# Wider tiles in two chained MoE layers behind a local attention, on one core

## The chip, the cores and the metric

One core of a Trainium2 chip runs the whole kernel. The metric is the device time of one execution in microseconds, launch to end; the kernel before was run three times. The profiled execution is a single one, and its span (first to last instruction) is a little shorter than its time.

## What is computed

Everything is float32. Attention: 4 batches, 8 heads, 768 tokens of 64 channels, in chunks of 32 queries; each chunk sees 16 tokens to its left, itself, 8 to its right and 8 memory tokens. Its output, 3072 tokens of 512 channels, goes through two feed-forward layers:

```python
h = x @ w_in                    # 512 -> 2048
x = (np.maximum(h, 0) ** 2) @ w_out          # -> 512
g, val = x @ w_gate, x @ w_val  # 512 -> 1536 each
out = (g / (1 + np.exp(-g)) * val) @ w_out2  # -> 512
```

## The kernel before

**Numbers as pairs.** A float32 operand is split into a high part in a format that TensorE takes at full rate (float32r) and a low remainder, and each product is three passes: high by high, high by low, low by high. The split is a copy on ScalarE and a subtraction on VectorE or GpSimd (`split`, L94). The weights come as 64-bit words and are put together on the chip first.

**First MoE.** The tokens are 32 groups of 96. They are worked on in blocks of `BLOCKS` groups (L29), eight blocks of 4, so 384 tokens, which are the columns that a matmul moves. A block goes over 16 tiles f of 128 hidden channels. Tile f has 12 matmuls for the hidden layer (`hidden_pe`, L368, matmul in L375; 4 channel groups by 3 passes), a relu and two squares on ScalarE and a subtraction on VectorE (`relu`, `square`, `square_again`, `square_lo`), and 12 matmuls that project back (`project_pe`, L410, matmul in L419). The hidden part of a tile runs two tiles ahead of its projection and alternates between two PSUM banks (`hbank`). At the end of a block the sums go through a `ys` tile to DRAM (`y1d`, L425 to L436).

**The clock of the program is the step.** Each tile has four steps of six matmuls, so a block has QB = 64, numbered through all blocks (`hs`). At the end of a step, `side(hs)` (L732) issues what is planned for it: first attention stages, then weight preparation. Within an engine the order is that of the program; SP issues all DMAs in that order and waits at each for its data and its buffer.

**Attention** runs in units of 96 queries, each one group of a later block. Units 0 to 7 and the beginning of unit 8 are in a written-out opening (`OPENING`), up to step 56, which the change leaves alone. After it, unit u has its last product (`at_pv`, L264, matmul in L272) and the split of its result at a step e, and its earlier stages at lags from the e of the unit before it (L294 to L319): load of q and k, scores on TensorE (`at_scores`, L137, matmul in L150), row maximum on VectorE, exponentials on ScalarE in two halves, normalising and 32x32 transposes on VectorE, load of v. For blocks from the second on, e is evenly spaced, 16 steps apart, and the last one is 15 steps before the block's end.

**Weight preparation for the second MoE.** That layer uses Strassen-like products: seven instead of eight 2x2 block products. So 18 chunks c of weights are loaded (`load2`), joined, combined on GpSimd (`prep_sums`, L464), split into pairs in three parts (`prep_split`, L476) and stored to DRAM as `w2d` (`prep_store`, L490). Chunk c starts at step a, about 16 steps apart from block 2 on (L717), with lags in `PREP` (L507).

**Second MoE.** It takes 2 x `NT2` tokens in a step s, with NT2 = 384 columns in a matmul, so `NS` = 4 steps. Its inputs come back from `y1d` (`load_z`), are combined and split (`sum_t`, `split_t`). Then 12 gated columns of 7 products of 6 matmuls (`gated`, L610; `product`, L599, matmul in L605), whose results VectorE and ScalarE turn into four u blocks in `uf` tiles; GpSimd forms sums of them (`sum_u`, L587). Then an output half of 42 items of 6 matmuls (`item_pe`, L647, matmul in L652), whose operands are split into a ring of `NRING` = 10 pairs ahead of time (`split_u`, L594), and whose seven sums are combined and stored (`combine`, L677). The 126 weight chunks of a step stream from `w2d` in groups of four (`load_chunks`, L515): when a group has been used, the load of the group five further on is issued (L608, L662).

Temporaries of the second MoE are `double()` tiles, six in rotation. `uf` tiles, weight tiles, the split inputs and the chunk groups share 16 buffers of 2048 floats a partition (pool `wp`).

Of the kernel before, what the change touches and what calls it, by code (L numbers as in the profile page):

```python
# [27 lines left out]
NTOK = B * S  # L28
BLOCKS = (4, 4, 4, 4, 4, 4, 4, 4)  # L29
NTM = GQ * max(BLOCKS)  # L30
NT2 = 384
RB = 2
CB = 2
P2 = 2
NEG = -3.0e38
# [12 lines left out]
NCH = GVC + WOC  # L48
NRING = 10
RAW = 2048  # L50
# [18 lines left out]
def attention_moe_moe_kernel(ctx, tc, att, v0, w1, w2, out):  # L69
# [220 lines left out]
    def at_split_x(u):  # L290
        at_x_hi(u)
        at_x_lo(u)

    STAGES = (  # L294
        (-8, at_load),
        (0, at_scores),
        (2, at_max),
        (3, at_exp_1),
        (5, at_exp_2),
        (7, at_norm),  # L300
        (8, at_turn_1),
        (8, at_load_v),
        (10, at_turn_2),
    )


# [4 lines left out]
    for t, n in enumerate(BLOCKS[1:], 1):  # L311
        for j in range(n):
            e = 13 * j + 12 if t == 1 else QB * (t - 1) + (j + 1) * QB // n - 15
            for lag, fn in STAGES:
                plan.setdefault(max(0, before + lag), []).append((lag, fn, nunit))
            plan.setdefault(e, []).append((100, at_pv, nunit))
            plan.setdefault(e + 1, []).append((101, at_split_x, nunit))
            before = e
            nunit += 1  # L319
# [170 lines left out]
    def prep_store(c, part):  # L490
# [15 lines left out]

    PREP = (  # L507
        (0, prep_words), (2, prep_join), (3, prep_sums), (4, prep_split, 0), (7, prep_split, 1), (8, prep_split, 2),
        (9, prep_store, 0), (10, prep_store, 1), (12, prep_store, 2),
    )  # L510

# [62 lines left out]
    def double():  # L574
        return up.tile([128, 2 * NT2], F32, tag="tmp", name="tmp", bufs=6)

    uf, ring = [], []
    SLOT = {"A11": 0, "A21": 1, "A12": 2, "A22": 3, "S3": 4, "S1": 1, "S2": 0, "S4": 2}
    ITEMS = ("A11", "A12", "S2", "S3", "A22", "S1", "S4")
    abanks = [*hbank, *yb1]  # L580
    pbank = [b[:, :, 0:NT2] for b in (abank, yb0)]

    def u_of(p, name):
        k = SLOT[name]
        return uf[p][:, k * NT2:(k + 1) * NT2]
# [13 lines left out]
    def product(n, z, to):  # L599
        whi, wlo = chunk(n)  # L600
        zh, zl = z
        m = 0
        for wt, x in ((whi, zh), (whi, zl), (wlo, zh)):
            for k in range(2):
                pe.matmul(to, wt[:, k * 128:k * 128 + 128], x[:, k], start=m == 0, stop=m == 5)  # L605
                m += 1
        if n % 4 == 3:
            load_chunks(n // 4 + 5)  # L608

# [46 lines left out]
    def item(s, j):  # L656
        n = NCH * s + GVC + j
        to = pbank[(7 * s + j // NP) % 2]
        for k in range(2):
            item_pe(s, j, k, [to[:, 0], to[:, 1]])  # L660
        if n % 4 == 3:
            load_chunks(n // 4 + 5)  # L662

    acc, ready = {}, []

    def double_k():
        return double().rearrange("p (k n) -> p k n", k=2)

# [8 lines left out]
    def combine(s, i):  # L677
        p = pbank[(7 * s + i) % 2]
        if i == 0:
            acc["x"] = double_k()  # L680
            act.copy(acc["x"], p)
        elif i == 2:
            dve.tensor_tensor(acc["x"], p, acc["x"], ALU.add)
        elif i == 3:
            acc["y"] = double_k()
            dve.tensor_tensor(acc["y"], p, acc["x"], ALU.add)
        else:
            o = double_k()
            if i == 4:
                dve.tensor_tensor(o, acc["y"], p, ALU.subtract)  # L690
            else:
                dve.tensor_tensor(o, p, acc["y" if i == 5 else "x"], ALU.add)
            if i == 5:
                dve.tensor_tensor(acc["x"], p, acc["x"], ALU.add)
            h, e = {1: (0, 0), 4: (1, 0), 5: (1, 1), 6: (0, 1)}[i]
            ready.append((s, h, e, o))
# [19 lines left out]
    for c in range(NC2):  # L716
        a = QB * (P2 + c // 4) + (4, 18, 32, 44)[c % 4]  # L717
        at(a - 11, load2, c)
        for lag, fn, *args in PREP:
            at(a + lag, fn, c, *args)  # L720
    for f, fn, *args in (
        (0, load_z, 0), (2, split_b1, 0, 0), (3, split_b1, 0, 1), (3, sum_t, 0, "T1"), (3, sum_t, 0, "T3"),
        (4, sum_t, 0, "T2"), (4, sum_t, 0, "T4"), (4, split_t, 0, "T2"), (5, split_t, 0, "T3"), (6, split_t, 0, "T1"),
        (7, split_t, 0, "T4"), (8, split_t, 0, "B22"),
        (9, load_chunks, 0), (10, load_chunks, 1), (11, load_chunks, 2), (13, load_chunks, 3), (14, load_chunks, 4),
    ):
        at(last + 4 * f + 2, fn, *args)
# [96 lines left out]
    ring += [[t[:, k] for t in halves] for k in range(KD)]  # L824
    for tags in (("gh", "gl"),) * 3 + (("r", "r"),):
        n = 3 if tags[0] == "gh" else 2
        ring.append([gp.tile([128, NTM], R, tag=tag, name="ring", bufs=n) for tag in tags])
    for _ in range(2):
        t = rawp.tile([128, WC], R, tag="cut", name="ring", bufs=CB)
# [24 lines left out]
    for k in range(2):  # L854
# [3 lines left out]
        if k == 0:  # L858
            combine(s, 5)
            for args in ready:  # L860
                store(*args)
        o = double_k()[:, 0:1]
        dve.tensor_tensor(o, to, acc["x"][:, k:k + 1], ALU.add)  # L863
# [71 lines left out]
```

## Time and profile before

| | |
|---|---|
| median of three runs | 1142.89 us (1142.75 to 1144.05) |
| the profiled execution | 1142.75 us |
| its span | 1141.0 us |
| TensorE busy | 1128.5 us, 8300 matmul records |
| VectorE, ScalarE, GpSimd busy | 717.4, 551.8, 328.1 us |
| DMA | 245.18 MB, 215 GB/s over the span |

A matmul here has two records, one of its weight load (PEld) and one of the matmul (PE). A record lasts from the start to the modelled end in the pipeline, so matmuls that follow each other closely overlap; the pace is the distance of their starts. Pieces of the chain of waits do not overlap, and their length is the time that they add. The first MoE ends at about 613 us of the span, and the second fills the rest.

### The profile page before, as it was taken

To read this page: it belongs to the slowest core of one execution; us is meant where nothing else is said; L and a number is where in the kernel's file an instruction comes from. 1 tells how busy PE (TensorE), PEld (TensorE's weight loads), DVE (VectorE), ACT (ScalarE), POOL (GpSimd) and SP (SyncE) were. 2 spreads that over 40 slices of the span, in tenths; PEclk is the share of its full clock that TensorE was granted. 3 is DMA by queue.
4 is the path that set the end of the run, shared out by engine and by line. 5 is a ranking of instruction groups with operands and counts; after the bars stand their busy time and mean duration, and the time that the engine had idled before them with its cause. 6 is when DMAs were issued, how large, how long until landed. Compare 5 with 4: busy or idle time off the path is not lost.

```text
span 1141.0 us, 21345 instructions
## 1 busy us (share of the span) xinstructions
PE 1128.5 (99%) x8300; PEld 1112.5 (98%) x8300; DVE 717.4 (63%) x1227; ACT 551.8 (48%) x1348; POOL 328.1 (29%) x305
## 2 busy tenths in 40 slices
PE   6999999999999999999999999999999999999998
PEld 6999999999999999999999999999999999999998
DVE  7897345656556565653233667956696667956664
ACT  5896546666666667574452223422253223612242
POOL 0000001453525435250000334423252333513342
PEclk9999999999999999999999999999999999999999
DMA  9731204547655476551254856787778787787771
GB/s 374 309 126 53 90 27 154 200 172 248 230 211 200 160 251 228 184 185 43 84 185 167 341 203 221 270 285 270 288 266 292 266 306 250 260 297 254 257 313 75
DMA packets 79829, 245.18 MB, mean 215 GB/s; under 512 B 6256, under 2 KB 50800, under 8 KB 59504
## 3 DMA queue, kind: packets, MB, share of 16 engines
q1 hardware_dynamic: 79728, 243.82, 59.6%
q8 instruction: 65, 1.06, 0.4%
q14 instruction: 36, 0.29, 0.1%
HBM read 198.18 MB, written 45.61 MB: 214 GB/s over the span
## 4 chain that ended last, share of the span: by engine, by line
PE 98%; DMA 1%; SPq 0%; DVE 0%; ACT 0%; issue 0%; ACTq 0%
PE hbank L375 24%; PE yb L419 24%; PE yb L605 15%; PE hbank L605 15%; PE abank L652 8%; PE yb L652 7%; PE abank L272 2%; PE abank L150 2%; PE hbank L210 1%; DMA first_v<-in_v_dram 1%; PE hbank L652 1%; PE yb L192 0%; SPq L125 0%; DVE x L287 0%; DVE tmp L863 0%
## 5 line engine op out<-in xcount | busy, mean ns | idle before, releaser
L375 PE MATMUL hbank<-x,w 128*128 128x384 f32 (+1 forms) x1548 | 292.5, 337 | 0.0
L375 PEld LDWEIGHTS hbank<-x,w 128*128 128x128 f32 x1548 | 272.2, 191 | 0.8 <-issue 0.2
L400 DVE TENSOR_TENSOR gl<-r,gh 128x384 fp32r<-128x384 f32 x128 | 87.0, 681 | 228.1 <-ACT r L394 227.9
L419 PE MATMUL yb<-gh,w 128*128 128x384 f32 x1024 | 205.0, 337 | 0.0
L419 PEld LDWEIGHTS yb<-gh,w 128*128 128x128 f32 x1024 | 178.7, 188 | 2.2
L99 POOL TENSOR_TENSOR ring<-uf,ring 128x384 fp32r<-128x384 f32 x72 | 81.1, 1126 | 283.5 <-ACT ring L96 143.7
L592 POOL TENSOR_TENSOR uf<-uf 128x384 f32<-128x384 f32 x96 | 106.1, 1116 | 123.6 <-DVE uf L644 123.6
L605 PE MATMUL hbank<-w,wst 128*128 128x384 f32 x720 | 138.3, 334 | 0.0
L605 PE MATMUL yb<-w,wst 128*128 128x384 f32 x720 | 138.3, 334 | 0.0
L383 ACT ACTIVATE r<-hbank 128x384 f32<-128x384 f32 x128 | 62.9, 491 | 131.4 <-PE hbank L375 130.9
L605 PEld LDWEIGHTS hbank<-w,wst 128*128 128x128 f32 x720 | 126.0, 188 | 0.0
L605 PEld LDWEIGHTS yb<-w,wst 128*128 128x128 f32 x720 | 126.0, 188 | 0.0
L474 POOL TENSOR_TENSOR wraw<-cut 128x256 f32<-128x256 f32 x36 | 26.5, 736 | 345.1 <-DVE sm L239 260.7
L419 PE MATMUL yb<-gl,w 128*128 128x384 f32 x512 | 113.2, 334 | 0.0
L96 ACT CAST ring<-uf 128x384 fp32r<-128x384 f32 x168 | 86.0, 512 | 51.3 <-PE yb L652 24.8
L643 ACT ACTIVATE tmp<-tmp 128x384 f32<-128x384 f32 x48 | 25.2, 526 | 172.7 <-DVE tmp L642 172.7
L419 PEld LDWEIGHTS yb<-gl,w 128*128 128x128 f32 x512 | 90.9, 188 | 0.0
L652 PE MATMUL abank<-ring,wst 128*128 128x384 f32 x504 | 89.6, 334 | 0.0
L652 PEld LDWEIGHTS abank<-ring,wst 128*128 128x128 f32 x504 | 87.6, 188 | 0.0
L226 ACT ACTIVATE prob<-abank,mx 96x72 f32<-96x72 f32 x224 | 67.6, 309 | 40.8 <-DVE mx L218 40.5
L253 DVE STREAM_TRANSPOSE pT<-prob 32x256 f32<-32x256 f32 x196 | 85.1, 434 | 2.5
L652 PE MATMUL yb<-ring,wst 128*128 128x384 f32 x468 | 83.2, 334 | 0.0
(125 smaller groups left out, 1504.8 us busy)
## 6 DMA issues: line engine op xcount, KB each, us to landing
wst<-w2d SPq DMA_DIRECT2D x124, 1024.0 KB, 4.7
wraw<-in_w_dram SPq DMA_DIRECT2D x34, 1024.0 KB, 6.4
qk<-in_att_dram SPq DMA_DIRECT2D x28, 464.0 KB, 5.4
w2d<-wraw SPq DMA_DIRECT2D x48, 256.0 KB, 2.5
v<-in_att_dram SPq DMA_DIRECT2D x28, 256.0 KB, 5.1
y1d<-ys SPq DMA_DIRECT2D x8, 768.0 KB, 4.3
w2d<-wraw SPq DMA_DIRECT2D x12, 512.0 KB, 3.0
zraw<-y1d SPq DMA_DIRECT2D x8, 768.0 KB, 7.7
```

Source lines behind the costliest of these rows:

```text
L96: act.copy(hi, src)
L99: lo_engine.tensor_tensor(lo, src, hi.bitcast(F32), ALU.subtract)
L226: act.activation(probs[u % 2][:, h, 0:WK], s["s"][:, r, i], AF.Exp, bias=s["mx"][:, r, i:i + 1], scale=SCALE, accum_out=s["sm"][:, h],)
L253: dve.transpose(pT[row:row + 32, :, 32 * c:32 * c + 32], probs[u % 2][32 * c:32 * c + 32, :, col:col + 32],)
L375: pe.matmul(hbank[f % 2][:, cols], wt[:, k * 128:(k + 1) * 128], x[:, k, cols], start=i == 0, stop=i == 3 * KD - 1,)
L383: act.activation(r, hbank[f % 2][:, 0:n], AF.Relu)
L400: dve.tensor_tensor(gl, g["r"], g["gh"].bitcast(F32), ALU.subtract)
L419: pe.matmul(ybank[e][:, 0:nt_of[t]], wt[:, c:c + 128], gtile[t, f][g], start=f == 0 and p == 0, stop=f == NF1 - 1 and p == 2,)
L474: pool.tensor_tensor(o, x, y, op)
L592: pool.tensor_tensor(u_of(p, o), u_of(p, x), u_of(p, y), op)
L605: pe.matmul(to, wt[:, k * 128:k * 128 + 128], x[:, k], start=m == 0, stop=m == 5)
L652: pe.matmul(to[k], wt[:, 128 * k:128 * k + 128], u, start=p == 0 and m == 0, stop=p == NP - 1 and m == 2,)
```

## The change

The second MoE takes 512 columns in a matmul (NT2), 1024 tokens in a step and so three steps. The first MoE has seven blocks of 4, 4, 5, 5, 5, 5 and 4 groups, so 384 or 480 columns. The steps of the attention units 8 to 31 (`UNIT_AT`), their lags (`UNIT_LAGS`), the starts of the 18 weight preparations (`PREP_AT`) and their lags (`PREP_LAGS`) become written-out lists; of the first unit in block 2 the stages beyond lag 2 move one step later. The u blocks of 512 columns fill their `uf` tiles with four, so the S3 sums get tiles of their own: one of the 16 `wp` buffers, which holds four of them, and two tiles that the first MoE used. For it the weight groups in flight go from five to four (`AHEAD`), the ring from ten pairs to nine, the temporaries from six to four, with one more for a running sum, and sums are written in place. The SBUF kept for descriptors of software DMAs shrinks to 2048 bytes.

```diff
@@ -26,12 +26,18 @@
 KD = DM // 128
 NF1, NF2 = FF1 // 128, FF2 // 128
 NTOK = B * S
-BLOCKS = (4, 4, 4, 4, 4, 4, 4, 4)
-NTM = GQ * max(BLOCKS)
-NT2 = 384
+UNIT_AT = (
+    65, 76, 90, 101, 114, 126, 138, 151, 164, 178, 190, 203, 215, 227, 240, 254, 267, 279, 291, 305, 321, 337,
+    353, 369,
+)
+UNIT_LAGS = (-8, 0, 1, 2, 5, 5, 6, 7, 5)
+PREP_LAGS = (-11, 0, 2, 2, 4, 7, 6, 9, 10, 11)
+BLOCKS = (4, 4, 5, 5, 5, 5, 4)
+NTM = 512
+NT2 = 512
 RB = 2
 CB = 2
-P2 = 2
+PREP_AT = (77, 102, 132, 146, 158, 178, 196, 212, 226, 238, 260, 270, 287, 300, 324, 340, 352, 364)
 NEG = -3.0e38
 SCALE = 1.0 / D ** 0.5
 NI = NH // 2
@@ -46,7 +52,8 @@
 NP = NF2 // 2
 GVC, WOC = 7 * NF2, 7 * NP
 NCH = GVC + WOC
-NRING = 10
+NRING = 9
+AHEAD = 4
 RAW = 2048
 PIECES = (((0, 0), (32, 32)), ((0, 32), (32, 64)), ((0, 64), (32, 96), (64, 32)))
 WC = 1024
@@ -291,18 +298,9 @@
         at_x_hi(u)
         at_x_lo(u)
 
-    STAGES = (
-        (-8, at_load),
-        (0, at_scores),
-        (2, at_max),
-        (3, at_exp_1),
-        (5, at_exp_2),
-        (7, at_norm),
-        (8, at_turn_1),
-        (8, at_load_v),
-        (10, at_turn_2),
-    )
-
+    STAGES = tuple(zip(UNIT_LAGS, (
+        at_load, at_scores, at_max, at_exp_1, at_exp_2, at_norm, at_turn_1, at_load_v, at_turn_2,
+    )))
 
     QB = 4 * NF1
     plan = {}
@@ -310,9 +308,9 @@
     before = -1
     for t, n in enumerate(BLOCKS[1:], 1):
         for j in range(n):
-            e = 13 * j + 12 if t == 1 else QB * (t - 1) + (j + 1) * QB // n - 15
+            e = 13 * j + 12 if t == 1 else UNIT_AT[nunit - 8]
             for lag, fn in STAGES:
-                plan.setdefault(max(0, before + lag), []).append((lag, fn, nunit))
+                plan.setdefault(max(0, before + lag + (t == 2 and j == 0 and lag > 2)), []).append((lag, fn, nunit))
             plan.setdefault(e, []).append((100, at_pv, nunit))
             plan.setdefault(e + 1, []).append((101, at_split_x, nunit))
             before = e
@@ -504,10 +502,10 @@
             for h, half in enumerate((hi.bitcast(F32), lo)):
                 sp.dma_start(out=place[:, :, h], in_=half[:, m * QC:n * QC].rearrange("p (n c) -> p n c", c=QC))
 
-    PREP = (
-        (0, prep_words), (2, prep_join), (3, prep_sums), (4, prep_split, 0), (7, prep_split, 1), (8, prep_split, 2),
-        (9, prep_store, 0), (10, prep_store, 1), (12, prep_store, 2),
-    )
+    PREP = tuple(zip(PREP_LAGS, (
+        (load2,), (prep_words,), (prep_join,), (prep_sums,), (prep_split, 0), (prep_split, 1), (prep_split, 2),
+        (prep_store, 0), (prep_store, 1), (prep_store, 2),
+    )))
 
     chunks = {}
     NS = NTOK // (2 * NT2)
@@ -572,15 +570,19 @@
         split(*zt[s][name], src, act, dve)
 
     def double():
-        return up.tile([128, 2 * NT2], F32, tag="tmp", name="tmp", bufs=6)
+        return up.tile([128, 2 * NT2], F32, tag="tmp", name="tmp", bufs=4)
 
     uf, ring = [], []
-    SLOT = {"A11": 0, "A21": 1, "A12": 2, "A22": 3, "S3": 4, "S1": 1, "S2": 0, "S4": 2}
+    SLOT = {"A11": 0, "A21": 1, "A12": 2, "A22": 3, "S1": 1, "S2": 0, "S4": 2}
     ITEMS = ("A11", "A12", "S2", "S3", "A22", "S1", "S4")
     abanks = [*hbank, *yb1]
     pbank = [b[:, :, 0:NT2] for b in (abank, yb0)]
 
+    s3 = []
+
     def u_of(p, name):
+        if name == "S3":
+            return s3[p]
         k = SLOT[name]
         return uf[p][:, k * NT2:(k + 1) * NT2]
 
@@ -605,7 +607,7 @@
                 pe.matmul(to, wt[:, k * 128:k * 128 + 128], x[:, k], start=m == 0, stop=m == 5)
                 m += 1
         if n % 4 == 3:
-            load_chunks(n // 4 + 5)
+            load_chunks(n // 4 + AHEAD)
 
     def gated(s, f, side):
         n0 = NCH * s + 7 * f
@@ -659,12 +661,12 @@
         for k in range(2):
             item_pe(s, j, k, [to[:, 0], to[:, 1]])
         if n % 4 == 3:
-            load_chunks(n // 4 + 5)
+            load_chunks(n // 4 + AHEAD)
 
     acc, ready = {}, []
 
-    def double_k():
-        return double().rearrange("p (k n) -> p k n", k=2)
+    def double_k(tile=None):
+        return (double() if tile is None else tile).rearrange("p (k n) -> p k n", k=2)
 
     def store(s, h, e, o, k0=0):
         t0 = (2 * s + h) * NT2
@@ -677,7 +679,7 @@
     def combine(s, i):
         p = pbank[(7 * s + i) % 2]
         if i == 0:
-            acc["x"] = double_k()
+            acc["x"] = double_k(up.tile([128, 2 * NT2], F32, tag="sum", name="sum"))
             act.copy(acc["x"], p)
         elif i == 2:
             dve.tensor_tensor(acc["x"], p, acc["x"], ALU.add)
@@ -685,7 +687,7 @@
             acc["y"] = double_k()
             dve.tensor_tensor(acc["y"], p, acc["x"], ALU.add)
         else:
-            o = double_k()
+            o = acc["y"] if i == 5 else acc["x"] if i == 6 else double_k()
             if i == 4:
                 dve.tensor_tensor(o, acc["y"], p, ALU.subtract)
             else:
@@ -714,15 +716,13 @@
 
     last = QB * (NB - 1)
     for c in range(NC2):
-        a = QB * (P2 + c // 4) + (4, 18, 32, 44)[c % 4]
-        at(a - 11, load2, c)
-        for lag, fn, *args in PREP:
-            at(a + lag, fn, c, *args)
+        for lag, (fn, *args) in PREP:
+            at(PREP_AT[c] + lag, fn, c, *args)
     for f, fn, *args in (
         (0, load_z, 0), (2, split_b1, 0, 0), (3, split_b1, 0, 1), (3, sum_t, 0, "T1"), (3, sum_t, 0, "T3"),
         (4, sum_t, 0, "T2"), (4, sum_t, 0, "T4"), (4, split_t, 0, "T2"), (5, split_t, 0, "T3"), (6, split_t, 0, "T1"),
         (7, split_t, 0, "T4"), (8, split_t, 0, "B22"),
-        (9, load_chunks, 0), (10, load_chunks, 1), (11, load_chunks, 2), (13, load_chunks, 3), (14, load_chunks, 4),
+        (9, load_chunks, 0), (10, load_chunks, 1), (11, load_chunks, 2), (13, load_chunks, 3),
     ):
         at(last + 4 * f + 2, fn, *args)
     lookahead = 2
@@ -822,9 +822,12 @@
     uf += [wp.tile([128, RAW], F32, tag="w", name="uf") for _ in range(NP)]
     halves = [xp.tile([128, KD, NTM], R, tag=f"x{i}", name=f"ring{i}") for i in range(2)]
     ring += [[t[:, k] for t in halves] for k in range(KD)]
-    for tags in (("gh", "gl"),) * 3 + (("r", "r"),):
+    for tags in (("gh", "gl"),) * 2 + (("r", "r"),):
         n = 3 if tags[0] == "gh" else 2
         ring.append([gp.tile([128, NTM], R, tag=tag, name="ring", bufs=n) for tag in tags])
+    t = wp.tile([128, RAW], F32, tag="w", name="s3")
+    s3 += [t[:, k * NT2:(k + 1) * NT2] for k in range(RAW // NT2)]
+    s3 += [gp.tile([128, NTM], F32, tag=tag, name="s3", bufs=3) for tag in ("gh", "gl")]
     for _ in range(2):
         t = rawp.tile([128, WC], R, tag="cut", name="ring", bufs=CB)
         ring.append([t[:, 0:NT2], t[:, NT2:2 * NT2]])
@@ -859,7 +862,7 @@
             combine(s, 5)
             for args in ready:
                 store(*args)
-        o = double_k()[:, 0:1]
+        o = acc["x"][:, k:k + 1]
         dve.tensor_tensor(o, to, acc["x"][:, k:k + 1], ALU.add)
         store(s, 0, 1, o, k)
     ordered.close()
@@ -921,7 +924,7 @@
     from concourse.bass_utils import run_bass_kernel_spmd as _run
 
     packed = _pack({n: _np.ascontiguousarray(a) for n, a in inputs.items()})
-    nc = _bacc.Bacc("TRN2", target_bir_lowering=False, num_devices=1)
+    nc = _bacc.Bacc("TRN2", target_bir_lowering=False, num_devices=1, dynamic_dma_scratch_size=2048)
     arrays, args = {}, []
     for name, a in packed.items():
         a = _np.ascontiguousarray(a)
```

## Rows read from the trace of the kernel before

**Rows 1.** The page: busy time by engine, and the granted clock in 40 slices.
```profile
PE 1128.5 (99%) x8300; PEld 1112.5 (98%) x8300; DVE 717.4 (63%) x1227; ACT 551.8 (48%) x1348; POOL 328.1 (29%) x305
...
PEclk9999999999999999999999999999999999999999
```
**Rows 2.** The chain that ended last, its shares of the span by engine and line.
```profile
by line: PE hbank L375 23.9%; PE yb L419 23.8%; PE hbank L605 15.3%; PE yb L605 15.3%; PE abank L652 7.7%; PE yb L652 7.1%; PE abank L272 2.0%; PE abank L150 1.7%; PE hbank L210 1.0%; DMA first_v<-in_v_dram 0.9%; PE hbank L652 0.5%; PE yb L
```
**Rows 3.** What TensorE waited for: us in total, times, longest; the first of six entries.
```profile
PE yb L150 <- DMA qk<-in_att_dram: 4.3, 1, 4.3
```
**Rows 4.** Chain in order of time (start, us, what): output half of the second MoE.
```profile
700.85 6.24 PE abank L652 x36
707.09 6.24 PE yb L652 x36
```
**Rows 5.** The same view in the first MoE: one repeat of its pattern.
```profile
133.50 2.30 PE yb L419 x12
135.79 2.08 PE hbank L375 x12
...
151.84 2.30 PE yb L419 x12
```
**Rows 6.** Stretches: busy us (instructions) of PE, PEld, DVE, ACT, POOL; clock, DMA share, GB/s.
```profile
35.17:36.77 1.60, 1.60 (x6) 1.60 (x6) 0.26 (x1) 1.60 (x3) 0.00 (x0) 1.00 1.06 417
...
50.00:150.00 100.00, 100.00 (x903) 97.11 (x902) 71.72 (x132) 71.47 (x192) 0.00 (x0) 1.00 0.24 83
...
350.00:450.00 100.00, 100.00 (x904) 97.24 (x903) 58.10 (x106) 64.52 (x181) 42.78 (x40) 1.00 0.62 217
...
700.00:800.00 100.00, 100.00 (x578) 100.00 (x578) 74.23 (x112) 35.81 (x71) 38.24 (x33) 1.00 0.78 275
700.85:744.53 43.68, 43.68 (x253) 43.68 (x253) 37.35 (x44) 22.01 (x41) 21.28 (x16) 1.00 0.78 271
```
**Rows 7.** TensorE in order of time (start, us), two windows that end one matmul apart.
```profile
34.72 0.97 PE L375 MATMUL hbank<-x,w 128*128 128x384 f32 x2
...
34.72 1.29 PE L375 MATMUL hbank<-x,w 128*128 128x384 f32 x3
```
**Rows 8.** Groups by line (count | busy, mean ns | idle before): weight loads of 128, 64, 32 columns.
```profile
L419 PEld LDWEIGHTS yb<-gh,w 128*128 128x128 f32 x1024 | 178.7, 188 | 2.2
...
L272 PEld LDWEIGHTS abank<-pT,v 128*64 128x64 f32 x448 | 19.4, 136 | 7.0 <-issue 5.7 <-DVE cut L358 0.5 <-DVE ys L435 0.5
...
L150 PEld LDWEIGHTS abank<-qk 64*32 64x32 f32 x1296 | 15.5, 106 | 3.2
```
**Rows 9.** In order of time: unit 9 on TensorE, ScalarE, VectorE and SP's queue.
```profile
114.42 0.74 PE L150 MATMUL abank<-qk 64*32 64x64 f32 x48
115.09 1.68 PE L419 MATMUL yb<-gh,w 128*128 128x384 f32 x8
...
122.17 0.20 ACT L226 ACTIVATION_READ_ACCUMULATOR prob<-abank,mx 96x1 f32 x1
...
122.84 0.75 DVE L244 TENSOR_TENSOR prob<-prob,sm 96x576 f32<-96x576 f32 x1
...
125.85 3.12 DVE L253 STREAM_TRANSPOSE pT<-prob 32x256 f32<-32x256 f32 x7
...
116.61 0.55 SPq L131 DMA_DIRECT2D v<-in_att_dram  x1
```
**Rows 10.** Groups by line: the VectorE add at 384 and at 768 columns.
```profile
L624 DVE TENSOR_TENSOR tmp<-hbank,tmp 128x384 f32<-128x384 f32 x24 | 13.4, 557 | 11.2 <-PE hbank L605 11.2
...
L692 DVE TENSOR_TENSOR tmp<-abank,tmp 128x768 f32<-128x768 f32 x6 | 5.7, 955 | 13.0 <-PE abank L652 13.0
```
**Rows 11.** In order of time: the last instruction of VectorE.
```profile
1137.69 0.56 DVE L863 TENSOR_TENSOR tmp<-hbank,tmp 128x384 f32<-128x384 f32 x1 [2.57 <-PE hbank L652]
```
**Rows 12.** The page: DMA issues, count, KB each, median us from issue to landing.
```profile
wst<-w2d SPq DMA_DIRECT2D x124, 1024.0 KB, 4.7
...
v<-in_att_dram SPq DMA_DIRECT2D x28, 256.0 KB, 5.1
```

## The prediction

> **What bounds the kernel now.** I read the page first. TensorE is busy for 1128.5 of 1141.0 us and its granted clock is full in every slice; VectorE, the next engine, has 63% [rows 1]. Busy matmuls overlap in a pipeline, so I went on to the chain of waits: 98% of it is TensorE, some 24% each for the two lines of the first MoE (L375, L419), 30.6% for L605 and 15.3% for L652 of the second [rows 2]. The third view, what TensorE waited for, is nearly empty: six entries, all in the opening with its first attention units, the longest 4.3 us [rows 3]. So the kernel is a string of matmuls at one pace, and only their pace, their number, or a new hole in the string can change the time.
>
> The pace is read where nothing else runs on TensorE. In the output half of the second MoE every 36 matmuls of 384 columns take 6.24 us [rows 4], 173.3 ns each. In the first MoE twelve take 2.08 us, the same 173.3, and the pattern repeats every 18.34 us [rows 5]: 96 matmuls (16.64 us) and one attention unit, which therefore costs 1.70 us of TensorE. Traffic does not move the pace: the first pieces lie in a stretch at 275 GB/s, the others begin in one at 83 [rows 6].
>
> **What a wider matmul costs** is the term that decides, and the trace has no 480- or 512-column form. At 2.4 GHz, 384 columns alone are 160.0 ns, so 13.3 ns of the 173.3 are something else. Early in the span, before the pace settles, the same form starts every 320 ns [rows 7] (1.29 less 0.97). That is one column per cycle at 1.2 GHz, the lower level by the pace, though the clock column prints full there [rows 6]. So columns can go through at one per cycle, and the 13.3 ns appear only at the upper level. Is it the weight load? Its records are 106 ns for 32 columns, 136 for 64, 188 for 128 [rows 8]: about 0.86 ns a column and 79 fixed, so 128 columns keep the load path busy for some 110 ns, less than 173. Three readings are left: (a) 13.3 ns per matmul, whatever its width; (b) 8.3% per column; (c) a floor of 173.3 which a longer matmul covers. For (a) speaks that no traffic shifts the excess and that at 1.2 GHz no column is slowed; (c) needs a load slower than rows 8 show. I take (a): 480 columns 213.3 ns, 512 columns 226.7. The bounds are (b), 216.7 and 231.1, and (c), 200.0 and 213.3.
> The Trainium skill (TensorE: Matmul & The Clock Gate, Back-to-back issue gap) gives N/2.4 plus a fixed 2.5 ns, which would be 162.5 ns at 384; the row says 173.3, so on the total the measurement decides. If only those 2.5 ns were per matmul, the saving worked out below would be 2.9 us instead of 15.2.
>
> **The change, part by part.** First MoE: eight blocks of 16 x 24 matmuls are 3072; seven are 2688. Columns stay the same (32 groups of 96), so 384 x 13.3 ns = **-5.1 us**. Second MoE: four steps of 126 x 6 = 756 are 3024, three are 2268; columns again stay (3024 x 384 = 2268 x 512), so 756 x 13.3 = **-10.1 us**. Three passes over the prepared weights instead of four save nothing more: no load is waited for now.
>
> Attention: 28 units at 1.70 us stay; they are moved and their stages drawn together. One place looks tight. Unit 9 gets its scores at step 65, as before, but its last product at step 76 instead of 81. In the trace [rows 9] the scores of step 65 begin at 114.42 and the next matmuls at 115.09; eleven steps of 1.04 us later is 126.5. The second half of its exponentials keeps its lag of 5 and ends by 122.4; normalising runs to 123.6; seven transposes take 3.12, so 126.7. TensorE would wait 0.2 us. The same gap at steps 90 to 101 starts after the hidden half of a tile, closer to the next relu group, and fits. In the 480-column blocks a step is 1.28 us, so the shortest gap there (12) is 15.4 us against this chain of 12.3. I take **+0.2**, with bounds of 0 and 24 such waits (+4.8). The v load moves up in SP's order by a step; in the trace it is issued at 116.61, ten us before 126.5 [rows 9], and lands in 5.1 [rows 12], so it costs nothing; a weight store that held SP in front of it would eat into those ten us first.
>
> Weight preparation: the same 18 with all their loads and stores, from step 66 instead of 121, up to 375; they are spread wider. Block 1 (steps 64 to 127) gets five units and two preparations beside 384 columns in 75 us; the blocks of before that lie in 350 to 450 us have four of each in 73, and there ScalarE is at 65 and VectorE at 58 of 100 while TensorE never pauses [rows 6]. So it is covered, and GpSimd was idle in that early stretch [rows 6]. The order of a preparation's parts (0, 2, 1 at lags 4, 6, 7) is seen by GpSimd and SP alone, where only later stores queue. If the cover failed, ScalarE would bring a relu late, and that has two tile times of slack, as each of the two banks is used every second tile.
>
> Buffers: nine ring pairs instead of ten hold 9 x 1.36 = 12.2 us of items, before 10 x 1.04 = 10.4. Four weight tiles instead of five are three groups of 24 matmuls ahead, 16.3 us (before four of 4.16, 16.6); a load lands in 4.7 [rows 12]. Four temporaries instead of six: a tile of one gated column is taken again a column later, when its last reader is past. All three at nothing. VectorE: a 384-column add takes 557 ns, a 768-column one 955 [rows 10], so 512 columns are about 690, 1.24 times, while a matmul grows 1.31 times. Its densest stretch, the output half with the next inputs' splits, 37.35 of 43.68 us [rows 6], becomes some 46 of 57: looser. GpSimd's sums grow by 512/384 at most, about like the pace.
>
> End: after the last matmul a 0.56 us add ends at 1138.25 [rows 11], and the store takes the 2.8 us that are left. The add becomes 0.69 and the store 256 KB instead of 192: +0.13, and between 0 and a third of 2.8; I take **+0.4** in all. The smaller DMA scratch I cost at nothing, as the data transfers stand in SP's own queue [rows 12].
>
> **Sum** against the profiled execution: -5.1 - 10.1 + 0.2 + 0.4 = -14.6, span 1126.4. That execution took 1142.75 us, 1.75 over its span, so 1128.1; it stands 0.14 under the median of the three runs, and I forecast **1128.2**.
>
> **Rivals.** *Per column* (b): the excess grows with the width and nothing is saved: 1142.9 + 0.6 = 1143.5. For it: 13.3 is one twelfth of 160 as neatly as it is a constant. Against it: at 1.2 GHz the columns run at full rate. Chance 8%.
> The rule of the Trainium skill cited above is a milder form of it and would give 1140.6.
> *Floor* (c): 1152 narrow matmuls keep their 13.3 ns and the other 4944 of now lose it: -65.9, so 1077.6. Against it: rows 8. Chance 4%.
> *Attention sets the pace* (slower): the drawn-together stages leave each last product waiting for its transposes (L272 on VectorE). It decides from 15.2/24 = 0.63 us per moved unit on; at 1.0 us each it is 24 - 14.8 = +9.2, so 1152. For it: unit 9 is already 0.2 over. Against it: three us of slack in the wide blocks. Chance 5%.
> *Part given back*: holes of 3 to 10 us in all, at block ends or where the second MoE starts, whose first input loads are 1 MB instead of 768 KB in front of ScalarE's splits: 1131 to 1138. Against it: there is not one such wait now [rows 3]. Chance 7%.
>
> **How the numbers follow.** The forecast has 76%. Within it an excess off by 2 ns on the 3804 wide matmuls is 7.6 us, so the range begins at 1121; it reaches to the end of the given-back case, 1138, and so holds about 83%. A difference under 0.2% (2.3 us) can't be told from none. Faster: 76 + 4 + 7 = 87%; same: 8%; slower: 5%.
>
> **What would show it.** Right: 36 output matmuls every 8.16 us, twelve of 480 columns in 2.56, and no entry beyond 1 us in TensorE's waits outside the opening. Wrong: 8.32 us for the 36 (b) or 7.68 (c); L272 waiting for VectorE or for v in block after block; L605 or L652 waiting for a weight tile, a ring pair or a gated result.

## The result and the profile after

The changed kernel takes 1131.28 us (median of 4 runs), before 1142.82: a ratio of 0.9902, 95% interval 0.9884 to 0.9919. It is faster by 11.5 us where 14.6 were forecast, and inside the range. The profiled execution has a span of 1129.8 us, 11.2 less.

The page of the changed kernel, beside [rows 1]:

```profile
PE 1116.8 (99%) x7160; PEld 966.3 (86%) x7160; DVE 705.6 (62%) x1059; ACT 532.5 (47%) x1212; POOL 317.5 (28%) x263
```

1140 matmuls fewer, as counted, and still TensorE from end to end. The weight loads, 98% before, leave gaps now. The chain in order of time, first in the output half of the second MoE, beside [rows 4], then in a 480-column block of the first, beside [rows 5]:

```profile
725.49 8.16 PE abank L654 x36
...
758.29 8.44 PE abank L654 x36
...
207.36 2.60 PE yb L417 x12
209.96 2.60 PE hbank L373 x12
```

At 512 columns 36 matmuls take 8.16 us, 226.7 ns each, to the digit the forecast. At 480 columns twelve take 2.60 us, 216.7 ns each, where 213.3 were forecast: that is 0.4514 ns a column, the 173.3/384 of before. The starts alternate in this kernel, about 212.5 and 220.8 ns apart. In each of the first two output halves one piece of 36 is longer, 8.44 and 8.41.

What TensorE waited for, beside [rows 3], is again the opening, where some of the smaller entries differ, and behind it one line:

```profile
PE abank L654 <- issue: 0.2, 1, 0.2
```

The span is cut at three places that both traces have: the start of unit 8's last product (step 65, all in the old blocks up to there), the first matmul of the second MoE, and the last matmul. All columns are in us. The kernels below the first two rows are those of the experiments, given here so that all can be read together.

| kernel | to unit 8's product | rest of first MoE | first to last start, second MoE | end |
|---|---|---|---|---|
| before | 113.61 | 499.72 | 523.99 | 3.72 |
| changed | 111.58 | 499.46 | 514.71 | 4.04 |
| changed, second profile | 114.87 | 499.46 | 514.73 | 4.05 |
| second MoE alone | 111.43 | 499.72 | 514.67 | 4.11 |
| first MoE alone | 115.14 | 499.45 | 525.59 | 3.79 |
| more splits on GpSimd | 111.13 | 499.47 | 517.25 | 4.05 |
| none on GpSimd | 110.74 | 499.44 | 513.89 | 4.04 |
| 512-column blocks, 1st | 114.55 | 500.19 | 514.69 | 4.05 |
| 2nd | 113.50 | 501.12 | 514.74 | 4.04 |
| 3rd, no splits on GpSimd | 113.83 | 498.24 | 513.90 | 4.04 |
| 4th, the same, units moved | 110.94 | 495.40 | 513.90 | 4.04 |

So the change is worth -0.3 in the first MoE, -9.3 in the second and +0.3 at the end, 9.2 us in all. The other 2.0 us lie ahead of step 65, where the change does no more than move some stages of unit 8 by one to four steps. They lie ahead of unit 4's last product even: from that to unit 8's both traces take 58.91 us. The piece of the chain with the first 40 hidden matmuls shows where, in the trace of before:

```profile
31.23 8.97 PE hbank L375 x40
```

and in that of the changed kernel:

```profile
31.03 7.15 PE hbank L373 x40
```

The same instructions: in the trace of before five starts of 384 columns lie 320 ns apart here, the pace of 1.2 GHz [rows 7], in that of the changed kernel none, and in its second profile 15. In eleven of the twelve profiles this piece is found whole; it takes from 6.53 to 10.47 us, and 7.15 and 10.43 in the two of the changed kernel. So it goes by the execution and not by the kernel. It accounts for most of the 4 us by which runs of one kernel differ, as far as the profiled runs show, and the columns behind it, which repeat within 0.1 us, decide what follows here.

### The profile page after: what moved, and what is told of

Same layout as the page of the kernel before. It is cut to its first block, busy times and chain, and to the rows that moved or that the text cites. A ratio compares the mean times of both kernels' runs of the same rounds, so it can differ in the third digit from the quotient of the medians.

```text
span 1129.8 us, 18416 instructions
## 1 busy us (share of the span) xinstructions
PE 1116.8 (99%) x7160; PEld 966.3 (86%) x7160; DVE 705.6 (62%) x1059; ACT 532.5 (47%) x1212; POOL 317.5 (28%) x263
## 4 chain that ended last, share of the span: by engine, by line
PE 99%; DVE 1%; DMA 0%; issue 0%; ACT 0%; ACTq 0%
PE hbank L373 24%; PE yb L417 24%; PE hbank L607 15%; PE yb L607 15%; PE abank L654 7%; PE yb L654 7%; PE abank L279 2%; PE abank L157 2%; PE hbank L217 1%; PE hbank L654 1%; DMA qk<-in_att_dram 0%; PE yb L199 0%; DVE first_p L177 0%; DVE mx L170 0%; PE yb L157 0%
## 5 line engine op out<-in xcount | busy, mean ns | idle before, releaser
L373 PE MATMUL hbank<-x,w 128*128 128x480 f32 (+3 forms) x1356 | 289.6, 361 | 0.0
L417 PE MATMUL yb<-gh,w 128*128 128x480 f32 (+1 forms) x896 | 201.2, 361 | 0.0
L398 DVE TENSOR_TENSOR gl<-r,gh 128x480 fp32r<-128x480 f32 (+1 forms) x112 | 77.7, 695 | 190.2 <-ACT r L392 189.6
L417 PEld LDWEIGHTS yb<-gh,w 128*128 128x128 f32 x896 | 162.5, 188 | 15.8
L106 POOL TENSOR_TENSOR ring<-uf,ring 128x512 fp32r<-128x512 f32 x51 | 71.7, 1407 | 274.4 <-ACT ring L103 274.4
L607 PE MATMUL hbank<-w,wst 128*128 128x512 f32 x540 | 132.6, 389 | 0.0
L607 PE MATMUL yb<-w,wst 128*128 128x512 f32 x540 | 132.6, 389 | 0.0
L417 PE MATMUL yb<-gl,w 128*128 128x480 f32 (+1 forms) x448 | 110.2, 359 | 0.0
L103 ACT CAST ring<-uf 128x512 fp32r<-128x512 f32 x108 | 67.1, 621 | 45.8 <-PE yb L654 21.0
L654 PE MATMUL abank<-ring,wst 128*128 128x512 f32 x360 | 83.3, 389 | 0.2 <-issue 0.2
L654 PE MATMUL yb<-ring,wst 128*128 128x512 f32 x360 | 83.3, 389 | 0.1
L654 PEld LDWEIGHTS abank<-ring,wst 128*128 128x128 f32 x360 | 67.5, 188 | 14.6 <-issue 0.6
```

The costliest lines, as they stand in the source:

```text
L103: act.copy(hi, src)
L106: lo_engine.tensor_tensor(lo, src, hi.bitcast(F32), ALU.subtract)
L373: pe.matmul(hbank[f % 2][:, cols], wt[:, k * 128:(k + 1) * 128], x[:, k, cols], start=i == 0, stop=i == 3 * KD - 1,)
L398: dve.tensor_tensor(gl, g["r"], g["gh"].bitcast(F32), ALU.subtract)
L417: pe.matmul(ybank[e][:, 0:nt_of[t]], wt[:, c:c + 128], gtile[t, f][g], start=f == 0 and p == 0, stop=f == NF1 - 1 and p == 2,)
L654: pe.matmul(to[k], wt[:, 128 * k:128 * k + 128], u, start=p == 0 and m == 0, stop=p == NP - 1 and m == 2,)
```

## The experiments

**One half of the change at a time.** The first kernel takes the first MoE back:

```diff
-BLOCKS = (4, 4, 5, 5, 5, 5, 4)
+BLOCKS = (4, 4, 4, 4, 4, 4, 4, 4)
...
```

The lines left out put the steps and lags of before into `UNIT_AT`, `UNIT_LAGS`, `PREP_AT` and `PREP_LAGS`.

> The change with the first MoE put back to eight blocks of 384 columns and with the units and preparations of before; only the second MoE moves 512 columns. Theory A (a 480-column matmul costs as much per column as a 384-column one, so the first MoE's new blocks gave nothing): within 1 us of the changed kernel, about 1131, some 10 us under before. Theory B (the forecast: the first MoE's part is worth 5 us and the missing 3 us were lost in holes or in the second MoE): about 1136, 5 us over the changed kernel.

Measured: 1134.41 us in the median of 4 runs (1131.63 to 1134.65), 0.9936 of before (0.992 to 0.9953). By the medians it is 3 us over the changed kernel, by the table it is not: 499.72 and 514.67 us against 499.46 and 514.71, so 0.2 us apart. The profile is that of the fastest run; that the three others lost their 3 us in the opening is inferred from the spread seen there. Theory A holds.

The second takes the second MoE back:

```diff
-NT2 = 512
+NT2 = 384
...
```

> The change with the second MoE put back to 384 columns (four steps, but nine ring pairs, four weight tiles and four temporaries as in the change). Theory A: no gain, within 1 us of before, 1142 to 1144, and the 480-column matmuls start alternately some 212 and 221 ns apart. Theory B: 1138. If the fewer buffers of the second MoE cost something by themselves, the time is over that of before and TensorE's waits show L607 or L654.

Measured: 1143.15 us in the median of 10 runs (1141.56 to 1145.67), 1.0015 of before (1.0003 to 1.0026). The seven blocks with all their new placements give 0.3 us (499.45), and twelve 480-column matmuls take 2.60 us here too. Theory A holds, and the forecast's 5 us are gone. But the second MoE, at the width of before, loses 1.6 us: in three of its four steps two starts at L654 lie about 0.6 us apart. The first place, and the output half around it, beside the last line of [rows 6]:

```profile
726.32 0.95 DVE L685 TENSOR_TENSOR sum<-abank,sum 128x768 f32<-128x768 f32 x1
...
727.37 1.45 PE L654 MATMUL abank<-ring,wst 128*128 128x384 f32 x7 [0.30 <-ACT w L103]
```

```profile
702.11:745.79 43.68, 43.38 (x250) 43.09 (x250) 39.67 (x44) 22.54 (x42) 23.12 (x17) 1.00 0.77 267
```

TensorE starts 0.1 us after the end of the sum (L685) on VectorE that read `abank`, and that sum is late. In the kernel before the same sum ends at 723.64, 2.0 us before the next items on its bank start:

```profile
722.70 0.94 DVE L683 TENSOR_TENSOR tmp<-abank,tmp 128x768 f32<-128x768 f32 x1
```

With as much to do at the same width VectorE is busy for 39.67 us instead of 37.35, and GpSimd for 23.12 instead of 21.28: with nine ring pairs nine splits of a half fall to GpSimd, with ten pairs eight. So what the change does to the second MoE beside the width is not free. Which part of it (ring, temporaries, sums in place) does this was not tried one by one.

**The width by itself.** A kernel of nothing but matmuls:

```python
WIDTHS = (512, 504, 496, 480, 464, 448, 432, 416, 400, 384, 352, 320, 288, 256, 192, 128, (480, 16), (480, 32), 512)
COUNT = 48
...
            for i in range(COUNT):
                pe.matmul(
                    banks[i // 12 % 4][:, 0:n], w[:, i % 8 * 128:i % 8 * 128 + 128], x[i % 2][:, at:at + n],
                    start=i % 12 == 0, stop=i % 12 == 11,
                )
```

> Only streams of 48 float32r matmuls with full weight loads at one width after the other (512, 504, 496, 480, 464, 448, 432, 416, 400, 384, 352, 320, 288, 256, 192, 128, then 480 with its moving operand 16 and 32 columns further on, then 512); nothing else of the layers is computed. Theory A (the alternation belongs to the width): 480 takes 217 ns on average here too, 512 takes 226.7 and 384 takes 173.3; the widths that are multiples of 128 show N/2.4 + 13.3, others more. Theory C (the alternation comes from the place of the operand in its tile, or from the work beside it): 480 takes 213.3 in this stream, at least with one of the three places. Reading (b) of the forecast: every width costs N/2.4 x 1.083.

Here are stretches that reach from the first matmul of one width to the first of the next (the length, then busy time and records of TensorE, its weight loads, VectorE, ScalarE and GpSimd; records over 48 lie at the edges):

```profile
42.98:53.38 10.40, 10.40 (x50) 9.01 (x49) 0.00 (x0) 0.00 (x0) 0.00 (x0) 1.00 0.00 0
21.37:32.26 10.89, 10.89 (x50) 9.02 (x49) 0.00 (x0) 0.00 (x0) 0.00 (x0) 1.00 0.01 2
...
63.40:73.12 9.72, 9.72 (x49) 9.02 (x48) 0.00 (x0) 0.00 (x0) 0.00 (x0) 1.00 0.00 0
91.57:100.21 8.64, 8.64 (x49) 8.64 (x48) 0.00 (x0) 0.00 (x0) 0.00 (x0) 1.00 0.00 0
```

The length over 48 is the pace: 480 columns 216.7 ns, 504 columns 226.9, 448 columns 202.5, 400 columns 180.0. All of them, with what is over one column per 2.4 GHz cycle:

| columns | 512 | 504 | 496 | 480 | 464 | 448 | 432 | 416 | 400 | 384 | 352 | 320 | 288 | 256 | 192 | 128 |
|---|---|---|---|---|---|---|---|---|---|---|---|---|---|---|---|---|
| ns | 226.7 | 226.9 | 223.3 | 216.7 | 208.8 | 202.5 | 196.0 | 188.3 | 180.0 | 174.0 | 161.0 | 146.7 | 131.9 | 119.8 | 111.2 | 111.0 |
| over | 13.3 | 16.9 | 16.7 | 16.7 | 15.4 | 15.8 | 16.0 | 15.0 | 13.3 | 14.0 | 14.3 | 13.3 | 11.9 | 13.1 | | |

The first 512-column matmuls of the stream start 427 ns apart, the pace of 1.2 GHz; the table gives the spacing after that. So the 216.7 ns belong to the width, as theory A says: they come without traffic and without another engine. The alternation does not: here the starts at 480 lie 215 to 218 ns apart, with the same mean. Placed 16 and 32 columns further on, 480 takes about 218, so theory C (213.3 at one of the places) is out. The excess is 13.3 ns at 512, 400, 320 and 256 and up to 17 between 416 and 504. Neither of the two readings is a rule for all widths. Reading (b), 8.3% per column, meets every width from 384 to 504 within 1 ns and misses 512 (231.1) by 4.4 and 256 (115.6) by 4.2; reading (a), 13.3 ns per matmul, meets 512 and those from 256 to 400 within 1.5. So 512 stands out among its neighbours rather than 480. Multiples of 128 are not what makes a good width (400 and 320 are none). At 192 and 128 columns a floor of 111 ns appears, near the weight load that the forecast put at some 110 [rows 8].

The next one asks whether the excess comes from the load, by halving it:

```diff
-w[:, i % 8 * 128:i % 8 * 128 + 128]
+w[:, i % 8 * 128:i % 8 * 128 + c]
```

Here c, the number of weight columns, is 128, 64 or 32.

> Only streams of 48 float32r matmuls again, moving 512, 480, 448 and 384 columns with weight loads of 128 columns and then of 64 (also 256 and 128 moving with 64, and 480 with 32); nothing of the layers is computed. Theory H (what is above one column per cycle comes from the weight load getting in between): with 64 weight columns the excess over N/2.4 at 480 falls from 16.7 ns to about a half or less, and at 512 from 13.3 likewise. Theory I (it belongs to the moving operand's width alone): 64 weight columns change nothing.

The stretches of 480 columns with 64 and with 32 weight columns:

```profile
62.08:72.63 10.55, 10.55 (x50) 6.52 (x49) 0.00 (x0) 0.00 (x0) 0.00 (x0) 1.00 0.00 0
...
99.00:109.40 10.40, 10.40 (x52) 5.26 (x50) 0.00 (x0) 0.00 (x0) 0.00 (x0) 1.00 0.00 0
```

Measured with 64 weight columns (with 128 in brackets): 512 columns 230.0 ns (226.7), 480 columns 219.8 (216.7), 448 columns 202.4 (202.7), 384 columns 173.2 (173.4); 480 columns with 32 weight columns take 216.7 again. Nothing falls at these widths, so theory H is out for them. Theory I holds at 448 and 384; the 3 ns more at 512 and 480 neither theory had. At 256 columns the pace falls, from 119.8 to 113.8, and 128 columns take 60.0, below the floor of before: there the load is in it. Why 480 costs 16.7 and 512 costs 13.3 stays open.

**The holes in the output half.** The piece of 8.44 us begins late by 0.3. What VectorE, GpSimd and TensorE did just before, in the changed kernel:

```profile
754.84 1.66 POOL L106 TENSOR_TENSOR ring<-uf,ring 128x512 fp32r<-128x512 f32 x1 [1.78 <-ACT ring L103]
...
755.27 1.78 DVE L106 TENSOR_TENSOR ring<-uf,ring 128x512 fp32r<-128x512 f32 x1
...
756.98 1.21 DVE L685 TENSOR_TENSOR sum<-abank,sum 128x1024 f32<-128x1024 f32 x1
...
758.11 0.68 DVE L106 TENSOR_TENSOR ring<-uf,ring 128x512 fp32r<-128x512 f32 x1
...
758.29 1.39 PE L654 MATMUL abank<-ring,wst 128*128 128x512 f32 x5 [0.16 <-issue]
```

TensorE starts again on `abank` 0.1 us after the combine (L685) that read it has ended, at 758.19. That combine could start when the chain went on to the items of the other bank, at 749.97. VectorE reached it only at 756.98: it is busy without a break from 744 to 760. The split before it took 1.78 us beside one on GpSimd; the same split alone takes 0.68. In the kernel before this was so too: of 24 splits on VectorE in a half eight take over 1.0 us, most of them 1.37, and the others mostly 0.54. Now it is 11 of 24, and 11 of 24 at 384 columns with the new buffers as well.

> The changed kernel with every second split of an output item on GpSimd instead of every fourth. Theory F (the two holes of the output half come from combines that VectorE reaches late): VectorE has some 8 us less to do in a half of 57, the starts of L654 more than 300 ns apart are gone, 0.8 us gained. Theory G (VectorE is late because its adds and GpSimd's hold each other up: 0.68 us alone, 1.78 beside one): more of its adds take 1.78 us, the holes stay or grow, the time is the same or up to 3 us longer.

```diff
-split_u, s, j, pool if j % 4 == 1 else dve
+split_u, s, j, pool if j % 2 == 1 else dve
```

Measured: 1136.38 us (1133.61 to 1136.95), and the second MoE 2.5 us longer, with two holes of 1.3 to 1.4 us. VectorE has eight splits fewer in an output half and is busy for longer: 53.2 us instead of 51.65, in a half that is itself longer, 58.8 us for 57.4. Theory G holds. Its opposite takes the splits off GpSimd:

```diff
-split_u, s, j, pool if j % 4 == 1 else dve
+split_u, s, j, dve
```

> The changed kernel with no split of an output item on GpSimd after the first ones: all on VectorE. Theory F (VectorE has too much to do): nine more adds in a half, the holes grow, the second MoE's matmuls take over 515.5 us from first to last start. Theory G (the adds beside GpSimd are what makes VectorE late): fewer adds of 1.78 us, VectorE busy for less than the 51.7 of 57.1 us of now, both holes gone, 513.9 us from first to last start instead of 514.7.

The output half, in the changed kernel

```profile
725.33:782.45 57.12, 56.96 (x252) 46.85 (x251) 51.65 (x44) 27.99 (x42) 28.83 (x17) 1.00 0.63 216
```

and without splits on GpSimd:

```profile
725.00:782.00 57.00, 57.00 (x253) 47.22 (x252) 49.08 (x53) 28.01 (x42) 14.49 (x8) 1.00 0.66 221
```

VectorE (the third engine of the row) has nine instructions more and is busy 2.6 us less (2.3, if the half is cut at its first matmul in both); TensorE is busy throughout. The second MoE takes 513.89 us, as theory G had said (513.9). Timed in more runs:

> The changed kernel with all item splits on VectorE, timed in rounds. Theory G: 0.8 us under the changed kernel for the same opening, so 1130 to 1133.5, and in the profile no start of L654 more than 300 ns after the one before.

Measured: 1130.55 us (1130.04 to 1133.1), 0.9909 of before (0.9894 to 0.9925), again 513.89 in the second MoE and no hole at L654.

**The changed kernel again**, to see what a second profile repeats:

> The changed kernel once more, nothing altered, beside the others on this chip. Theory E (runs differ by when the clock of TensorE rises in the opening): its time is 1131 to 1134, and in its profile the first unit's product on abank (L279) starts between 52 and 57 us, while from there to the last matmul it takes the same as before, within 0.3 us.

Measured: 1133.22 us (1130.93 to 1134.83); the first unit's product starts at 55.95 us, 3.3 later than in the first profile, and the other columns of the table agree within 0.02. Theory E holds. Beside it the kernel before took 1142.58 (11 runs), so here the change is worth 9.4 us, close to the 9.2 of the table.

**Wide blocks in the first MoE too.** If only paces count, 512-column blocks must pay where 480-column ones did not.

```diff
-BLOCKS = (4, 4, 5, 5, 5, 5, 4)
+BLOCKS = (4, 4, 5, 6, 5, 5, 3)
+WIDTHS = (384, 384, 480, 512, 512, 512, 288)
...
```

The lines left out place units and give a unit whose tokens lie in two blocks its high and low parts in two pieces.

> The changed kernel with first-MoE blocks of 384, 384, 480, 512, 512, 512 and 288 columns; a 512-column block does not end at a group of 96 queries, so units 18 and 23 write their result into two blocks, and units 13 to 31 are placed anew. Priced with the paces measured so far (173.3, 216.7, 226.7 and 131.8 ns; 384 matmuls a block): 2 x 66.6 + 83.2 + 3 x 87.0 + 50.6 = 528.0 us against 3 x 66.6 + 4 x 83.2 = 532.5 in the changed kernel. Theory A (only the paces count): 4.5 us under the changed kernel, about 1126.7. Theory D (units 11 steps apart and results split between blocks make TensorE wait): L279 or L373 in TensorE's waits with some us, and no gain.

Measured: 1135.13 us (1131.72 to 1135.86), 0.9928 of before (0.9912 to 0.9944), and 0.7 us more than the changed kernel in the first MoE. In its waits stand two lines that the changed kernel does not have:

```profile
PE hbank L386 <- ACT x L303: 2.7, 1, 2.7
...
PE yb L430 <- DVE ys L446: 1.6, 1, 1.6
```

The first is unit 23 at the end of a block, whose split stood behind a mask on VectorE and a preparation on ScalarE; the second a finished block's copy behind unit 14's exponentials. They are 4.3 us; without them it would be 495.9. The next version moved both and three preparations:

> The version with three 512-column blocks again, with the two places mended where TensorE waited: unit 13 at step 126 instead of 124, so that its exponentials don't stand in front of the copy of a finished block, units 14 to 17 two steps later, unit 23 a step sooner, and three preparations 4 to 6 steps sooner. Theory A: from unit 8's product to the second MoE 495 us, against 499.5 in the changed kernel and 500.2 in the first attempt (which had 4.6 us of waits). Theory D (a result split between two blocks makes TensorE wait whatever is moved): a wait of 1 us or more on L303 stays, 497 us or more.

Measured: 501.12 us in the first MoE, worse (1135.14 us in all, one run). The two waits are gone, and three new ones stand at the last products of units 15, 16 and 23. The worst, in order of time on TensorE, and the stretch behind it:

```profile
237.06 0.88 PE L292 MATMUL abank<-pT,v 128*64 128x96 f32 x16 [1.82 <-issue]
...
238.53 4.44 PE L386 MATMUL hbank<-x,w 128*128 128x480 f32 x12
```

```profile
237.00:242.00 5.00, 4.95 (x73) 4.24 (x74) 3.86 (x6) 0.48 (x1) 0.06 (x1) 0.66 0.54 156
```

After a pause of some 2 us the granted clock is 0.66 of full on average in these 5 us, and twelve matmuls take 4.44 us for 2.60: seven of them start 400 ns apart, which is 480 columns at 1.2 GHz. A wait of two us cost close to four.

The third version loads v four steps earlier, to have no weight store in front of it on SP, puts preparations 9 to 13 behind unit 23, and takes the splits off GpSimd:

> The version with three 512-column blocks and no item splits on GpSimd, its two places of waiting mended in another way: v is loaded four steps earlier in SP's order, so that no weight store stands in front of it, unit 23 is at step 245 again, and preparations 9 to 13 start 2 to 8 steps later, behind that place. Theory A (only the paces count once nothing waits): 495 us from unit 8's product to the second MoE and 513.9 in it, 5.3 us under the changed kernel for the same opening, 1126 to 1129 by the clock's rise. Theory D: waits of 1 us or more on L293 or L304 stay, and the first MoE keeps 497 us or more.

Measured: 1131.83 us, 0.9913 of before (0.9899 to 0.9926), 498.24 in the first MoE. Units 15 and 16 still wait, 0.9 and 1.9 us, though v is issued earlier. So SP was not it: seven transposes end at 219.45 and 237.34, and the products start 0.1 us after each. At unit 15 ScalarE's second exponentials begin at 213.77, behind the relu and squares of a tile. If that is the reason, the chain of a unit depends on the step within a tile at which it starts, and other steps must mend it:

```diff
-126, 137, 148, 159, 170, 181,
+125, 135, 146, 157, 168, 181,
```

> The version before, with units 13 to 18 at 125, 135, 146, 157, 168 and 181 instead of 126, 137, 148, 159, 170 and 181. Theory D' (what was left, 2.8 us at units 15 and 16, is the chain from scores to transposes, whose second exponentials stand behind a relu group, and so depends on the step within a tile at which it starts): both waits go, 495.4 to 495.8 us from unit 8's product to the second MoE, and 513.9 in it; 1124.5 to 1129 by the clock's rise. Rival: with three preparations beside six units in one block VectorE and ScalarE are simply late there, wherever the units stand: the waits move to other units, 497 us or more.

Measured: 1126.16 us (1125.83 to 1129.14), 0.9868 of before, interval 0.9849 to 0.9887. First MoE 495.40, second 513.90, both as said beforehand, and no wait of TensorE is left behind the opening but unit 9's 0.1 us. The rival, that the waits move to other units, is out. This beats both kernels: 4.9 us under the changed one where no opening counts (4.1 and 0.8 by the table).

## Why the prediction was right, and where it was not

- *What bounds the kernel*: right. All of the gain behind the opening is fewer matmuls, each with its excess.
- *512 columns at 226.7 ns*: right, and with it -10.1 us for the second MoE but for 0.8. That part was lost at two steps. One put the new buffers at nothing: by the experiment at 384 columns they, with the order that they bring and without a wider matmul, take VectorE from 37.35 to 39.67 of 43.68 us and make its sums late. In the kernel before VectorE was already busy without a break from 713 to 727 us, which the average of the half hides. The other step called that densest stretch looser, "some 46 of 57": it is 51.65 of 57.12, and from 39.67 that is 1.30 times, like the pace, not 1.24. The scaling to an add of 690 ns holds for an add alone (0.68 to 0.69); what it left out is the splits beside GpSimd, which grow from 1.37 to 1.78 us. Without output splits on GpSimd the forecast's number comes out, 513.9.
- *480 columns at 213.3 ns*: wrong, and the largest error. "13.3 ns per matmul, whatever its width" held for 512 and failed for 480, where it is 16.7. 1536 matmuls by 3.3 ns is 5.1 us, all that the first MoE was to give. The bound (b) for 480, 216.7, is what came, and (b) at every width from 384 to 504; but the rival (b) was priced for both widths at once, so the forecast had no case in which one width gains and the other does not. The measured time lies in the range as the range reached to 1138 for holes, not for this.
The Trainium skill's rule (TensorE: Matmul & The Clock Gate, Back-to-back issue gap), N/2.4 and 2.5 ns, is met by no width here: it makes 215.8 of 512 columns, and the stream shows 226.7.
- *Unit 9 waits 0.2*: right in kind, 0.11 (382 ns from the last matmul to its product, where 268 is usual). *End +0.4*: 0.3.
- *Preparation and v at nothing*: right for this kernel; the table shows the first MoE in two profiles at 499.46 with no other hole.
- *Not in the sum at all*: the opening, 2.0 us better by chance in the profiled pair. Its rows were read for the pace [rows 7], but not for the spread that it gives to every run; a range from several runs would have shown it. This was luck: it hid part of the miss, which is 3.4 us by the spans and 5.4 (9.2 for 14.6) where no opening counts.
- *The rival that attention sets the pace* did not come here. In two of the wide-block versions two or three units waited, 0.8 to 1.9 us each, where the rival had put 1.0 at all 24.

## What to carry to other kernels

Before a matmul is widened, measure its pace at that very width in a short stream: here one width (512) gave 2% a column and a near one (480) nothing. Change buffers and width one at a time: at the old width the new buffers and their order already made VectorE late. Where two engines hold each other up, taking work off the late one can make it later; count its busy time, not its instructions. And compare kernels between marks that both traces have, so that an opening that varies does not hide a gain of a few us.

## What the runs showed of the hardware that was not expected

- The pace of a float32r matmul is not linear in its width: 504 columns cost as much as 512 (226.9 and 226.7 ns), and 400 take 180.0 nearly every time. At 480 the mean is 216.7 whether the starts alternate between 212.5 and 220.8 (the changed kernel) or lie 215 to 218 apart (the stream).
- Halving the weight columns makes some wide matmuls slower and none of 384 columns or more clearly faster: 219.8 for 216.7 ns at 480, 230.0 for 226.7 at 512, 202.4 for 202.7 at 448; with a quarter of them 480 takes 216.7 again.
- A subtraction of 128x512 on VectorE takes 0.68 us alone and up to 1.78 beside one on GpSimd; with nine fewer on GpSimd and nine more on VectorE, VectorE is busy for 2.3 to 2.6 us less in 57.
- A pause of about 2 us was followed by the lower clock in one run (0.66 over 5 us); a like pause at the same place in the third wide version was not (1.00 over 237 to 242 us). Why is open.
